# Local masks on VectorE, v's copies two half-steps later, and the third batch's scores in one group for each pair

## The chip, the core and the metric

The kernel runs on one core of a Trainium2 chip. The metric is the device time of one execution in microseconds, and the median over runs is what is compared. In this text PE is TensorE, DVE is VectorE, ACT is ScalarE, POOL is GpSimd and SP is SyncE, as the profile names them. One profiled execution supplies all times inside the kernel; they are counted from the start of its span.

## What is computed

Sparse attention over 8 batches of 8 heads (576 positions, head size 64) is followed by a two-layer block over the 4608 tokens. Heads 0 to 3 are local: a query sees its own key and the 31 before it. Heads 4 to 7 are strided: a query sees the earlier keys at its own position modulo 32.

```
scores = scale * q @ k.T                       # per batch and head
local   = (rel >= 0) & (rel < 32)              # heads 0..3, rel = query - key
strided = (rel >= 0) & (key % 32 == query % 32)  # heads 4..7
attn = softmax(where(mask, scores, -1e9));  x = attn @ v   -> (4608, 512)
h = x @ w_in                                   # 512 -> 2048
g = where(h > 0, h, exp(min(h, 0)) - 1)
out = g @ w_out                                # 2048 -> 512
```

## The kernel before, in words

**Two streams in one instruction order.** The two-layer block is done in 9 chunks of 512 tokens. Chunk `nb` has 16 steps `s`. A step multiplies 512 tokens by 128 columns of `w_in` (`moe_in`, four matmuls at L672), applies the activation (`moe_act`: the exponential on ACT at L698, then L705 and L707 on DVE), and does a quarter of one output block of `w_out` (`moe_out`, four matmuls at L721, mostly for the chunk before). The attention of batch `nb + 1` is laid between these pieces while chunk `nb` runs. Places between pieces are called gaps: gap `2s` is ahead of `moe_in` of step `s`, gap `2s + 1` is behind its `moe_act` and ahead of `moe_out`. The order on each engine is the order of emission, and an engine runs its instructions in that order.

**Opening and second batch.** The first batch is computed ahead of chunk 0 by a list, `OPENING`. The second batch (`b = 1`) lies in chunk 0 by the list `SECOND` of gap numbers and steps; `S0`, `S1` are its strided pairs of heads, `l0`, `l1` its local pairs. `t_q` and `t_k` are PE transposes with a copy out of PSUM, `s0`, `s1` the two halves of the scores, `a0`, `a1` the two halves of the product with v, `x` the transposition of the result into `xT`, and `halo` a copy inside v's local tile. `ON_VECTOR` names the copies that run on DVE; the others run on ACT.

**Later batches.** The third batch (`b = 2`, in chunk 1) follows `TIMES[2]`, whose pairs begin at gaps 4, 10, 15 and 21, strided pairs first. The offsets in the last tuple are for `t_q`, `t_k`, first scores, second scores, first product with v, second product, `x`, and `v_in`. `v_in` copies the strided v from `v_raw`, where a DMA has put it, to `v_str` in two parts on DVE (L439); only the first pair of a batch does it. For `b = 2` the transposes still run on PE; from `b = 3` they are DMA transposes.

**Scores and masks.** With `b < WHOLE`, `scores(u)` computes half of a pair's blocks into the two banks of `pair_a`, takes one exponential over them and, for `b = 2`, multiplies by the mask on DVE (`mask`, L556). With `b >= WHOLE`, `scores_all` computes all blocks of a pair at once, in `pair_a` and in two more banks of the ring; it takes one exponential (L488) and one mask product (L490) over `pair_a`, and `scores_rest` a gap later takes two short exponentials (L502) and one short mask product (L505) over the two other banks. For `b = FAR = 1` the mask is not a product: a matmul of the identity with `far_s` or `far_l` writes a large negative number to the masked places (L524), and the scores are added to it.

**Banks.** PSUM has 8 banks: the pair `pair_a`, two for `moe_in` (`half`), and four `single`. In chunk 1 three singles form the ring from which transposes, rest banks, products with v and `x` are taken in turn, and the fourth collects `moe_out`. `moe_in` of step `s + 2` needs the bank that L707 of step `s` has read.

**Loads.** q, k, v and the weights are loaded by DMAs that POOL issues. The order behind the opening is: the rest of `w_in`, four pieces of `w_out` (L790), then `load_batch(2)` (strided q, k, v at L192 and L196, then local q, k, v), then the memsets and `load_batch(3)`.

Of the kernel before, what the change touches and what calls it, by code (L numbers as in the profile page):

```python
# [11 lines left out]
BF16 = mybir.dt.bfloat16  # L12
I32 = mybir.dt.int32
ALU = mybir.AluOpType
# [10 lines left out]
LB = 96  # L25

L_RUN = 6
NEG = -1e30
# [5 lines left out]
TIMES = (  # L34
    None,
    None,
    ((4, 10, 15, 21), 0, (-3, -2, 0, 2, 4, 6, 9, 0)),
    ((2, 9, 15, 22), 0, (-2, -1, 0, 2, 3, 5, 8, 0)),
    ((2, 8, 15, 22), 0, PIECES),
)  # L40
# [3 lines left out]

SECOND = """
3 S0.t_k 5 S1.t_k 7 S0.s0 9 S0.s1 11 S1.s0 11 S0.a0 12 S0.a1 13 S1.s1 14 S1.a0 14 l0.t_q
16 S0.x 17 l0.t_k 17 S1.a1 19 l0.s0 19 l1.t_q 20 S1.x 20 S1.halo 21 l0.s1 21 l1.t_k 23 l1.s0
24 l0.a0 25 l0.a1 25 l1.s1 27 l1.a0 28 l0.x 28 l1.a1 31 l1.x
""".split()

# [4 lines left out]
s0.a0 l0.m1 l1.s0 s1.a1 s0.a1 s1.halo fill.1 l1.s1 l1.m0 l0.a0 fill.1 s1.x l1.m1 l0.a1 s0.x  # L55
fill.1 l1.a0 l1.a1 moe.2 l0.x moe.3 S0.t_q l1.x S1.t_q moe.0 moe.1
""".split()
ON_VECTOR = "s0.t_q s1.cast_q s1.t_k l0.t_q s0.v l1.x S1.t_q L1.t_k".split()


ON_SCALAR = (5, 7, 11, 15)
# [4 lines left out]
def kernel(  # L66
# [9 lines left out]
    nc = tc.nc  # L76
# [12 lines left out]
    consts = ctx.enter_context(tc.tile_pool(name="consts", bufs=1))  # L89
# [49 lines left out]
    identity = consts.tile([128, 128], BF16, tag="identity")  # L139
    mask_l = consts.tile([128, S], BF16, tag="mask_l")  # L140
    mask_w = consts.tile([128, 2 * 126 + 3 * 108], BF16, tag="mask_w")
    far_l = consts.tile([128, 3 * LB], BF16, tag="far_l")
    far_s = consts.tile([128, 126], BF16, tag="far_s")
    mask_s, mask_s3 = mask_w[:, 0:252], mask_w[:, 252:576]
    rden = consts.tile([128, B, 2, 2, 2, 6], F32, tag="rden")
# [25 lines left out]

    BY_DMA = 3

    WHOLE = 3

    FAR = 1
    RAW = 1
# [102 lines left out]
    for i in range(2):  # L280
# [19 lines left out]
                            op0=ALU.is_ge)  # L300
# [4 lines left out]
    for g in range(3):  # L305
# [8 lines left out]
                                   op0=ALU.is_le, op1=ALU.mult)  # L314
# [5 lines left out]

    nc.vector.tensor_scalar(far_s[0:126], mask_s[0:126, 0:126], scalar1=1.0,
                            scalar2=-NEG, op0=ALU.subtract, op1=ALU.mult)
    nc.vector.tensor_scalar(far_l, mask_l[:, 0:3 * LB], scalar1=1.0, scalar2=-NEG,
                            op0=ALU.subtract, op1=ALU.mult)

    load_strided(0, "k")
    load_local(0, "q")
# [26 lines left out]
    class Pair:  # L354
# [7 lines left out]
        def copy(self, step, late):  # L362

            if self.b < 2:
                name = self.name.upper() if self.b else self.name
                late = f"{name}.{step}" in ON_VECTOR
            return nc.vector.tensor_copy if late else nc.scalar.copy
# [139 lines left out]
        def scores(self, u):  # L507
            if self.b >= WHOLE:
                (self.scores_rest if u else self.scores_all)()
                return  # L510
            sc = rings["sc"].next()
            blocks = self.blocks(u)
            far = self.b == FAR
            if far:
                k, n = blocks[0][4:]
                g = len(blocks) // 2
                if self.strided:
                    t = far_s[0:k, 0:n].unsqueeze(1).to_broadcast([k, g, n])
                elif u == 0:
                    t = far_l  # L520
                else:
                    t = far_l[:, n:2 * n].unsqueeze(1).to_broadcast([k, g, n])
                for bank in range(2):
                    nc.tensor.matmul(sc[:, bank, 0:g * n], lhsT=identity[0:k, :],  # L524
                                     rhs=t, start=True, stop=False)
            for p, blk, bank, i, nk, nq in blocks:
                at, half = self.place(p, blk)
                d = slice(64 * half, 64 * half + 64)
                kind = "str" if self.strided else "loc"
                c = 0 if self.strided else LB * blk  # L530

                nc.tensor.matmul(sc[:, bank, i * nq:(i + 1) * nq],  # L532
                                 lhsT=kT[kind][self.b % 2][d, at, c:c + 128],
                                 rhs=qT[kind][self.b % 2][d, at, c:c + nq],
                                 start=not far,
                                 stop=not far or i == len(blocks) // 2 - 1)
            nk, nq = blocks[0][4:]
            w = len(blocks) // 2 * nq
            pr = (p_p if self.b else p_p0).tile([128, 1152 if self.b else 648], BF16, tag="pr", name="pr")
            halves = pr[0:nk, 0:2 * w].rearrange("k (a x) -> k a x", a=2)  # L540
            nc.scalar.activation(halves, sc[0:nk, :, 0:w], ACT.Exp, scale=scale)  # L541
            self.pr[u] = pr
            if self.b and not far:
                self.mask(u)
# [15 lines left out]
        def av(self, u):  # L560
# [8 lines left out]
            for p, blk, bank, i, _, _ in blocks:  # L569

                if self.b >= WHOLE:
                    pr, o, top = self.pr_all, self.probs[p, blk], 1152
# [70 lines left out]
    def attention(b, start, pitch, at):  # L643
# [6 lines left out]
        for i, pr in enumerate(pairs):  # L650
            for off, piece in ((at[0], pr.t_q), (at[1], pr.t_k),
                               (at[7], lambda pr=pr: pr.v_in(0)),
                               (at[7] + (b > 1), lambda pr=pr: pr.v_in(1)),
                               (at[2], lambda pr=pr: pr.scores(0)),
                               (at[3] if b < WHOLE else at[2] + (b < LATE),
                                lambda pr=pr: pr.scores(1)),
# [353 lines left out]
```

## Time and profile before

| What | Value |
|---|---|
| Median of 3 runs | 321.9 us (320.77, 321.9, 321.96) |
| Profiled execution, its own time | 322.11 us |
| Its span | 320.3 us |
| Granted PE clock | 0.997 |
| Busy: PE / DVE / ACT / POOL | 301.2 / 242.1 / 173.1 / 134.8 us |
| PE busy in 24.0 to 52.8 us | 26.70 of 28.80 us |
| PE busy in 52.8 to 88.0 us | 33.42 of 35.20 us |
| PE busy in 88.0 to 122.0 us | 33.78 of 34.00 us |

The profiled execution's own time is 1.8 us more than its span, which counts from the first to the last instruction. Chunk 0 of the two-layer block, with the second batch in its gaps, ends on PE at 52.84 us, where the first `moe_in` of chunk 1 starts; the third batch's attention lies in the gaps between there and 90.56 us, where chunk 2 starts. A duration in the tables of groups is the mean of one instruction. Matmuls follow one another faster than a single one lasts, so what a group of matmuls takes on PE is read from the start of its first to the start of what follows.

### The profile page before, as it was taken

How to read it: one execution, taken by the hardware profiler on the slowest of the kernel's cores; microseconds unless marked ns; L12 is line 12 of the kernel's file. 1: busy time of each engine (PE TensorE's matmuls, PEld its weight loads, DVE VectorE, ACT ScalarE, POOL GpSimd, SP SyncE). 2: the span in 40 equal slices, each digit the busy share in tenths (PEclk: the TensorE clock that was granted, in tenths of full speed). 3: DMA queues.
4: the chain of work that ended last, by engine and by line, in shares of the span. 5: the costliest groups of instructions: out<-in, count | busy, mean ns of one | idle time of the engine just before them, and what ended most of it. 6: DMA issues, size and time to landing. Idle time of an engine off the chain costs nothing.

```text
span 320.3 us, 6081 instructions
## 1 busy us (share of the span) xinstructions
PE 301.2 (94%) x2207; PEld 151.1 (47%) x2248; DVE 242.1 (76%) x542; ACT 173.1 (54%) x330; POOL 134.8 (42%) x213
## 2 busy tenths in 40 slices
PE   1899989899999999999999999999999999999994
PEld 0564545345444544444444544444445444444443
DVE  7787787487888988988798889887988666776610
ACT  3677876567455555456655655555565444434411
POOL 9666726959979658859733920000000000000000
PEclk9999999999999999999999999999999999999998
DMA  5999999999999999999997992571110000110012
GB/s 108 153 176 147 166 206 133 163 122 174 110 182 153 148 184 149 111 135 168 159 168 76 160 195 58 70 153 64 51 51 35 34 35 33 52 48 36 33 68 73
DMA packets 108971, 36.33 MB, mean 113 GB/s; under 512 B 87358, under 2 KB 104454, under 8 KB 108934
## 3 DMA queue, kind: packets, MB, share of 16 engines
q0 software_dynamic: 71632, 18.10, 63.7%
q1 hardware_dynamic: 37301, 17.77, 27.6%
q8 instruction: 19, 0.31, 0.4%
q14 instruction: 19, 0.15, 0.1%
HBM read 36.70 MB, written 9.44 MB: 144 GB/s over the span
## 4 chain that ended last, share of the span: by engine, by line
PE 78%; DMA 9%; DVE 6%; POOL 4%; issue 1%; ACT 1%; POOLq 0%; DVEq 0%; ACTq 0%
PE single L721 36%; PE half L672 25%; PE single L672 9%; DMA w_out_sb<-in_moe_w_out_dram 5%; PE single L577 3%; DMA k_loc<-in_k_dram 2%; PE pair_a L482 2%; DVE g_sb L707 2%; DMA v_raw<-in_v_dram 2%; DVE e_sb L705 1%; POOL k_str L192 1%; PE single L615 1%; PE single L400 1%; DVE x_l L588 1%; POOL w_out_sb L790 1%
## 5 line engine op out<-in xcount | busy, mean ns | idle before, releaser
L721 PE MATMUL single<-w_out_sb,g_sb 128*128 128x512 bf16 (+1 forms) x574 | 143.5, 373 | 1.1 <-issue 0.2
L672 PE MATMUL half<-xT,w_in_sb 128*128 128x512 bf16 x422 | 110.4, 379 | 1.9 <-DVE g_sb L707 1.1
L698 ACT ACTIVATE e_sb<-half 128x512 f32<-128x512 f32 x109 | 65.2, 599 | 73.5 <-PE half L672 70.4
L705 DVE TENSOR_SCALAR e_sb<-e_sb 128x512 bf16<-128x512 f32 x140 | 62.1, 444 | 35.5 <-ACT e_sb L698 34.8
L721 PEld LDWEIGHTS <-g_sb 128*128 128x128 bf16 x592 | 54.7, 98 | 56.2
L672 PEld LDWEIGHTS <-w_in_sb 128*128 128x128 bf16 x576 | 52.4, 98 | 57.5 <-issue 2.1
L707 DVE TENSOR_TENSOR g_sb<-e_sb,half 128x512 bf16<-128x512 bf16 x106 | 72.9, 688 | 3.7
L672 PE MATMUL single<-xT,w_in_sb 128*128 128x512 bf16 x133 | 35.8, 379 | 0.4
L698 ACT ACTIVATE e_sb<-single 128x512 f32<-128x512 f32 x35 | 21.1, 602 | 24.3 <-PE single L672 20.3
L726 ACT COPY o_sb<-single 128x512 f32<-128x512 f32 (+1 forms) x37 | 21.2, 574 | 17.3 <-PE single L721 16.9
L577 PEld LDWEIGHTS <-pr 128*128 128x128 bf16 (+3 forms) x352 | 20.7, 105 | 14.1 <-DVE pr L556 1.2
L488 ACT ACTIVATE pr<-pair_a 126x936 bf16<-126x936 f32 (+1 forms) x20 | 19.2, 962 | 11.9 <-PE single L482 11.9
L192 POOL DMA_DIRECT2D v_raw<-in_v_dram x32 | 20.0, 657 | 11.9 <-DVE v_str L439 11.7
L707 DVE TENSOR_TENSOR g_sb<-e_sb,single 128x512 bf16<-128x512 bf16 x34 | 23.4, 688 | 1.2
L192 POOL DMA_DIRECT2D k_str<-in_k_dram x32 | 19.6, 625 | 7.8 <-issue 3.1
L192 POOL DMA_DIRECT2D q_str<-in_q_dram x28 | 17.5, 643 | 5.5 <-DMA w_out_sb<-in_moe_w_out_dram 1.9
L588 DVE TENSOR_TENSOR x_l<-single,rden 96x384 bf16<-96x384 f32 x32 | 17.7, 553 | 1.1
L588 DVE TENSOR_TENSOR x_s<-single,rden 126x256 bf16<-126x256 f32 (+1 forms) x32 | 15.7, 491 | 1.1
L215 POOL DMA_DIRECT2D q_loc<-in_q_dram x20 | 15.7, 825 | 1.9 <-DMA k_str<-in_k_dram 1.9
L215 POOL DMA_DIRECT2D k_loc<-in_k_dram x20 | 15.3, 800 | 0.7 <-issue 0.4
L541 ACT ACTIVATE pr<-pair_a 128x576 bf16<-128x576 f32 (+2 forms) x20 | 13.0, 650 | 3.7 <-PE pair_a L532 3.5
L587 DVE RECIPROCAL rden<-single 96x6 f32<-96x6 f32 (+2 forms) x64 | 11.8, 185 | 2.4 <-PE single L577 1.9
(118 smaller groups left out, 254.9 us busy)
## 6 DMA issues: line engine op xcount, KB each, us to landing
out_dram<-o_sb SPq DMA_DIRECT2D x35, 256.0 KB, 2.6
v_loc<-in_v_dram POOLq DMA_DIRECT2D x8, 288.0 KB, 8.2
k_str<-in_k_dram POOLq DMA_DIRECT2D x32, 67.5 KB, 5.1
v_raw<-in_v_dram POOLq DMA_DIRECT2D x32, 67.5 KB, 5.0
w_in_sb<-in_moe_w_in_dram POOLq DMA_DIRECT2D x4, 512.0 KB, 8.0
w_out_sb<-in_moe_w_out_dram POOLq DMA_DIRECT2D x4, 512.0 KB, 12.5
q_str<-in_q_dram POOLq DMA_DIRECT2D x28, 67.5 KB, 6.9
q_loc<-in_q_dram POOLq DMA_DIRECT2D x20, 64.0 KB, 5.1
```

The costliest lines, as they stand in the source:

```text
L192: engine.dma_start(out=t[0:108, h].rearrange("p g d -> p (g d)"), in_=rows[h, :, 0:30, :].rearrange("t (r g) d -> t r (g d)", g=5))
L215: nc.gpsimd.dma_start(out=t[:, h // 2, 0:4, h % 2], in_=src[name][b, h, 0:512].rearrange("(i p) d -> p i d", p=128))
L488: nc.scalar.activation(both, sc[0:nk, :, 0:w], ACT.Exp, scale=scale)
L541: nc.scalar.activation(halves, sc[0:nk, :, 0:w], ACT.Exp, scale=scale)
L577: nc.tensor.matmul(to[:, 0:D] if apart else to, lhsT=pr[0:nk, o:o + m], rhs=vt[0:nk, 2 * self.hp + p, blk, :], start=True, stop=True)
L588: nc.vector.tensor_tensor(self.x[0:nq, b0:b0 + n].rearrange("q g p d -> q p g d"), av[0:nq, :, 0:n, 0:D], r.unsqueeze(3).to_broadcast([nq, ...
L672: nc.tensor.matmul(hps, lhsT=w_in_sb[:, c, m * 128:(m + 1) * 128], rhs=xT[:, c, nb * N_TILE:(nb + 1) * N_TILE], start=start, stop=stop)
L698: nc.scalar.activation(e_sb, hps, ACT.Exp)
L705: nc.vector.tensor_scalar(e1_sb, e_sb, scalar1=1.0, scalar2=1.0, op0=ALU.min, op1=ALU.subtract)
L707: nc.vector.tensor_tensor(g_of[nb][:, m, :], e1_sb, hps, op=ALU.max)
L721: nc.tensor.matmul(ops, lhsT=g_of[nb][:, m, kk * 128:(kk + 1) * 128], rhs=w_out_sb[:, m, cols], start=(m == 0), stop=(m == MC - 1))
L726: nc.scalar.copy(o_sb, ops)
```

## The change

Six things are different. `far_l` and the matmuls with it are gone, so that the second batch's local pairs get their mask by `mask` on DVE, as the third batch's do; its strided pairs keep `far_s`. `l1.t_k` of the second batch (`L1.t_k`) leaves `ON_VECTOR`, and its copy runs on ACT. `S1.x` and `S1.halo` move from gap 20 to gap 21. The third batch's `v_in` moves from offsets 0 and 1 to 2 and 3, which is from gaps 4 and 5 to gaps 6 and 7. `WHOLE` goes from 3 to 2, so that the third batch's scores go through `scores_all` and `scores_rest`. The tile `far_l` and the instruction that fills it are no longer there.

```
-    ((4, 10, 15, 21), 0, (-3, -2, 0, 2, 4, 6, 9, 0)),
+    ((4, 10, 15, 21), 0, (-3, -2, 0, 2, 4, 6, 9, 2)),
...
-16 S0.x 17 l0.t_k 17 S1.a1 19 l0.s0 19 l1.t_q 20 S1.x 20 S1.halo 21 l0.s1 21 l1.t_k 23 l1.s0
+16 S0.x 17 l0.t_k 17 S1.a1 19 l0.s0 19 l1.t_q 21 S1.x 21 S1.halo 21 l0.s1 21 l1.t_k 23 l1.s0
...
-ON_VECTOR = "s0.t_q s1.cast_q s1.t_k l0.t_q s0.v l1.x S1.t_q L1.t_k".split()
+ON_VECTOR = "s0.t_q s1.cast_q s1.t_k l0.t_q s0.v l1.x S1.t_q".split()
...
-    WHOLE = 3
+    WHOLE = 2
...
-    nc.vector.tensor_scalar(far_l, mask_l[:, 0:3 * LB], scalar1=1.0, scalar2=-NEG,
-                            op0=ALU.subtract, op1=ALU.mult)
...
-            far = self.b == FAR
+            far = self.b == FAR and self.strided
             if far:
                 k, n = blocks[0][4:]
                 g = len(blocks) // 2
-                if self.strided:
-                    t = far_s[0:k, 0:n].unsqueeze(1).to_broadcast([k, g, n])
-                elif u == 0:
-                    t = far_l
-                else:
-                    t = far_l[:, n:2 * n].unsqueeze(1).to_broadcast([k, g, n])
+                t = far_s[0:k, 0:n].unsqueeze(1).to_broadcast([k, g, n])
```

More of the change, by code (lines that the diff above doesn't have):

```diff
@@ L141 @@
     mask_w = consts.tile([128, 2 * 126 + 3 * 108], BF16, tag="mask_w")
-    far_l = consts.tile([128, 3 * LB], BF16, tag="far_l")
     far_s = consts.tile([128, 126], BF16, tag="far_s")
```

## The prediction

> **What bounds the kernel now.** I read the page's shares first, then the chain of work that ended last, in order of time, up to 66 us, then the timelines of PE and DVE over the same stretch, and last the groups of instructions by form. The shares of the chain:
>
> ```profile
> PE 78%; DMA 9%; DVE 6%; POOL 4%; issue 1%; ACT 1%; POOLq 0%; DVEq 0%; ACTq 0%
> ```
>
> Behind 64 us the chain is PE alone, matmul behind matmul. So a microsecond taken from PE there is a microsecond of the end, and one taken before is worth only what the last wait before 64 us lets through. That wait is in the chain (start, length, what):
>
> ```profile
> 36.49 15.22 DMA w_out_sb<-in_moe_w_out_dram
> ...
> 56.23 5.45 DMA v_raw<-in_v_dram
> ...
> 61.80 0.29 DVE v_str L439
> 62.09 0.33 DVE pr L556
> 62.42 0.35 DVE e_sb L705
> ...
> 62.79 0.70 DVE g_sb L707
> ...
> 63.53 0.38 PE half L672
> ```
>
> The third batch's v lands at 61.68 us, behind the weights, and its copy stands first on DVE, with a mask and an activation queued behind it. PE's and DVE's timelines show the same from both sides (the bracket is the idle time before):
>
> ```profile
> 55.23 0.43 PE L386 MATMUL single<-identity,k_str 126*128 126x126 bf16 x5 [0.23 <-DMA k_str<-in_k_dram]
> 62.48 0.33 PE L577 MATMUL single<-v_str,pr 126*128 126x65 bf16 x4 [0.67 <-DVE pr L556]
> 63.53 1.02 PE L672 MATMUL half<-xT,w_in_sb 128*128 128x512 bf16 x3 [0.46 <-DVE g_sb L707]
> 61.80 0.29 DVE L439 COPY v_str<-v_raw 126x512 bf16<-126x512 bf16 x1 [3.27 <-DMA v_raw<-in_v_dram]
> ```
>
> Two landings are thus dates that PE can't pass: 55.23 us for the key transposes, and v's. DVE sat idle for 3.27 us with work behind it. The prices come from the groups by form (busy, mean ns):
>
> ```profile
> L524 PE MATMUL pair_a<-far_l,identity 128*128 128x288 bf16 x8 | 1.6, 286 | 0.0
> L556 DVE TENSOR_TENSOR pr<-pr,mask_l 128x576 bf16<-128x576 bf16 x8 | 3.6, 450 | 0.0
> L403 DVE COPY kT_loc<-single 128x576 bf16<-128x576 bf16 x1 | 0.8, 751 | 0.0
> L488 ACT ACTIVATE pr<-pair_a 126x936 bf16<-126x936 f32 x10 | 9.5, 950 | 8.9 <-PE single L482 8.9
> L502 ACT ACTIVATE pr<-single 108x108 bf16<-108x108 f32 x20 | 4.0, 259 | 0.0
> L490 DVE TENSOR_TENSOR pr<-pr,mask_w 126x936 bf16<-126x936 bf16 x10 | 6.5, 646 | 5.1 <-ACT pr L488 5.1
> ```
>
> **The second batch, in chunk 0 (38 to 53 us).** PE loses four pairs of far_l matmuls. A pair holds PE for 0.34 us (39.29 to 39.63 us, and 41.85 to 42.19 us), so 1.36 us go, 0.34 of them ahead of a score matmul that waited 0.47 us for the key copy anyway. DVE gains four masks at 0.450, 1.80 us, and loses the key copy of 0.751: 1.05 us more. ACT gains that copy, 0.65 us at its own rate (L403 on ACT, 647 ns), ahead of the next exponential. I walked the three queues on from 38.4 us. PE first runs ahead by up to 1.1 us; then x of the first local pair waits for its normalisation, and the second half of the last pair's product with v waits for its mask at 48.85 us, where before it started at 48.83. The masks give back what the matmuls saved, and chunk 1 starts near 52.8 us, as before. The bounds are 51.5 us (all 1.36 kept) and 53.9 us (DVE's 1.05 all on PE). Either way little of it reaches the end: an early PE waits at 55.23 us for the keys, and a late one has 0.23 us there and some 0.65 us ahead of the product with v. I take 0, and a loss of 0.2 us at the late bound. S1.x at gap 21 takes away a 0.30 us wait for x_s (PE, 40.83 us), in the same cover. The filling of far_l (526 ns on DVE at 6.35 us) is hidden: PE's next steps there end on a landing of local keys at 13.86 us.
>
> **The first strided pair of the third batch (55 to 64 us).** From 55.23 us on I lay the new order out with the old durations. All scores at gap 4 take 0.36 us (the fourth batch's, 92.38 to 92.74 us) where two halves took 0.21 and 0.24. The exponential (0.95) and the mask (0.65) end at 59.4 us, the activation of step 2 at 60.5, the short mask at 60.8. DVE then stands before the copy of v from 60.8 to 61.8 us, with only step 3's activation behind it, whose exponential ends near 61. PE is at its first product with v at 61.5 us and waits for the copy alone: 61.80 + 0.29 + 0.06 gives 62.15 us instead of 62.48. The moe_in behind it needs the bank of step 2, which was free at 63.5 us and is now at 60.5, so the 0.46 us go too: 62.15 + 0.59 gives 62.74 us instead of 63.53. **Gain 0.79 us.** The second copy of v, at gap 7, stands behind step 3's activation and ends near 63.4 us; the second product with v comes at 64.4. The next product's normalisation follows it by 0.6 us.
>
> **The other three pairs (64 to 82 us).** Here PE is without waits, so its own time counts. Halves cost 0.45 (strided) or 0.46 us (local: 71.82 to 72.06 and 74.10 to 74.33), a group 0.36 (also local, 105.47 to 105.83): 0.1 each, 0.3 us. Ahead of a score group four large matmuls take 0.96 instead of 0.86 us (91.42 to 92.38 us against 93.61 to 94.47); the local pairs have one such place fewer each, 0.2 us. **Gain 0.5 us**, with bounds 0 and 0.75 (the last if the copies' slower products, 210 against 196 ns, go as well). ACT gets 0.95 + 2 times 0.26 where it had 0.59 and 0.71 us: 0.17 us a pair, beside idle time of over 1 us in six steps of that stage. DVE has the same elements in as many instructions.
>
> **Sum:** 322.11 - 0.79 - 0.5 = 320.8 us for the profiled execution, which stands 0.2 us above its median; for the median 321.9 - 1.3 = 320.6 us.
>
> **The rivals.** *The landings come earlier.* If PE's gain in chunk 0 holds and the landings aren't fixed dates, 1.36 + 0.30 us come on top: 319.0 us. For it: DMA share is 0.67 at 52 to 56 us, so the engines have room there. Against it: POOL is busy for 3.95 of those 4.00 us, and it issued k's remainder only when w_out had landed.
>
> *Nothing is gained, because v lands later.* The weights and loads ahead share the queues with outputs, and the profile can't say how fixed 61.68 us is. A microsecond later, plus a wait for a normalisation at gap 21, eats 1.3 us: 321.9 us. At gap 21 the first local pair's second product takes the bank of its first; before, that one was normalised at 79.22 us and PE came at 79.27.
>
> *VectorE locks GpSimd out.* Masks and copies on DVE would hold up POOL's writing of descriptors, so that v lands later by the four masks' 1.80 us: 322.11 + 1.80 - 1.29 = 322.6 us. Against it: in 37 to 52 us POOL waited for landings for some 10 us, which hides 1.8, and a mask beside busy POOL took 0.45 us (73.68 us) as one alone did. The Trainium skill (SBUF — State Buffer, "two separate sides") says that a DVE instruction in a two-port mode keeps GpSimd from writing DMA descriptors; copies in SBUF are of that kind, products of two tensors are not except against a GpSimd read. By that rule v's copies alone would matter, and they come when v's own issues are over.
>
> *Slower: two moe_in banks run short behind each group.* A long exponential and a long mask stand ahead of the activation that frees a bank. Behind the fourth batch's first group L707 ended at 95.73 us and its bank was needed at 96.33: 0.60 us to spare. In chunk 1, ACT has besides two copies out of PSUM for each pair (0.63 to 0.69 us) and the output copy (0.58 us), and the ring gives seven banks a pair instead of five. If both copies and an output copy fall between, 1.9 - 0.6 = 1.3 us are short, four times 5.2 us, or 2.6 us if at every second pair: 322.1 - 1.3 + 2.6 = 323.4, up to 326.0 us. It decides from L707 coming over 0.60 us later than there. Against it: the copies fall ahead of the pair's own group, a gap or more before.
>
> **How the numbers follow.** Measurements of this kernel tell about 0.5%, 1.6 us. The forecast (gain 0.5 to 2) gets 0.47, of which 0.15 lie beyond 1.6 us; earlier landings 0.20, nearly all of it beyond; nothing gained 0.12; the lock 0.05; slower by short banks 0.16, nearly all beyond 323.5 us. So faster 0.35, same 0.49, slower 0.16. The range, 319.0 to 323.4 us, leaves out the lower half of earlier landings and the upper half of short banks; the likeliest case alone has 319.9 to 321.4.
>
> **What would show it.** Right: no L524 with far_l; DVE's wait for v_raw falls from 3.27 to about 1 us and stands between the short mask and L439; PE's wait at the first product with v is for v_str, 0.3 to 0.7 us; the 0.46 us before moe_in is gone; PE waits about 0.2 us for k_str near 55.2 us. Wrong: chunk 1 starting after 53.7 us, v landing off 61.7 us by more than 0.5, or waits of moe_in for g_sb between 64 and 90 us.

## The result, and the profile after

The changed kernel's median is 319.67 us (22 runs, 318.57 to 322.71) against 321.41 us for the kernel before (22 runs, 319.99 to 322.54); the ratio is 0.9959 with a 95% interval of 0.994 to 0.9978. That is 1.3 us by the ratio and 1.7 us by the medians; forecast were 1.3 us and a ratio of 0.996. The profiled execution took 318.57 us, the fastest of its 22, where the one of before had taken 322.11 us, 0.7 us above its median. So the two profiles stand further apart (3.5 us) than the kernels do, and below every reading is made over several profiles.

The shares of the chain, from the page of the changed kernel:

```profile
PE 84%; DMA 6%; DVE 3%; POOL 2%; ACT 2%; issue 1%; POOLq 0%; ACTq 0%
```

PE has six points more, at the cost of DMA, DVE and POOL. PE's timeline has the same three places as before (start, length, work, and in brackets idle time ahead, of which there is none now):

```profile
54.01 0.44 PE L383 MATMUL single<-identity,k_str 126*128 126x126 bf16 x5
...
60.21 0.29 PE L569 MATMUL single<-v_str,pr 126*128 126x65 bf16 x4
60.34 0.43 PE L383 MATMUL single<-identity,k_str 126*128 126x126 bf16 x5
60.61 1.03 PE L664 MATMUL half<-xT,w_in_sb 128*128 128x512 bf16 x4
```

No 0.23 us for the keys, no 0.67 us at the product with v, no 0.46 us ahead of moe_in. DVE's timeline shows why:

```profile
57.51 0.65 DVE L487 TENSOR_TENSOR pr<-pr,mask_w 126x936 bf16<-126x936 bf16 x1 [0.38 <-ACT pr L485]
58.17 0.67 DVE L697 TENSOR_SCALAR e_sb<-e_sb 128x512 bf16<-128x512 f32 x1
58.87 0.69 DVE L699 TENSOR_TENSOR g_sb<-e_sb,half 128x512 bf16<-128x512 bf16 x1
59.48 0.26 DVE L502 TENSOR_TENSOR pr<-pr,mask_w 108x216 bf16<-108x216 bf16 x1
59.66 0.33 DVE L436 COPY v_str<-v_raw 126x512 bf16<-126x512 bf16 x1
```

Mask, activation and short mask now lie where DVE idled for 3.27 us, and the copy of v starts without a wait: v has landed by the time DVE comes to it. Chunk 0 has the local masks at the price that was taken from before, and the cost that the walk through the queues had found, x of the first local pair waiting for its normalisation (groups by form, and PE's timeline):

```profile
L548 DVE TENSOR_TENSOR pr<-pr,mask_l 128x576 bf16<-128x576 bf16 x8 | 3.6, 450 | 0.7 <-ACT pr L533 0.6
```

```profile
47.62 0.30 PE L620 MATMUL single<-identity,x_l 96*128 96x96 bf16 x3 [0.43 <-DVE x_l L580]
```

### The profile page after: what moved, and what is told of

Its sections match the earlier page's. It is cut to its first block, busy times and chain, and to the rows that moved or that the text cites. A ratio compares the mean times of both kernels' runs of the same rounds, so it can differ in the third digit from the quotient of the medians.

```text
span 316.8 us, 6114 instructions
## 1 busy us (share of the span) xinstructions
PE 299.8 (95%) x2240; PEld 149.1 (47%) x2240; DVE 242.6 (77%) x544; ACT 172.9 (55%) x335; POOL 137.5 (43%) x213
## 4 chain that ended last, share of the span: by engine, by line
PE 84%; DMA 6%; DVE 3%; POOL 2%; ACT 2%; issue 1%; POOLq 0%; ACTq 0%
PE single L713 39%; PE half L664 28%; PE single L664 9%; PE single L569 3%; DMA q_str<-in_q_dram 3%; PE pair_a L479 2%; DMA v_raw<-in_v_dram 2%; DMA k_str<-in_k_dram 2%; PE single L607 1%; ACT e_sb L690 1%; POOL k_str L191 1%; PE single L397 1%; DVE g_sb L699 1%; PE single L383 1%; DVE x_l L580 1%
## 5 line engine op out<-in xcount | busy, mean ns | idle before, releaser
L713 PE MATMUL single<-w_out_sb,g_sb 128*128 128x512 bf16 (+1 forms) x592 | 145.9, 373 | 0.0
L664 PE MATMUL half<-xT,w_in_sb 128*128 128x512 bf16 x436 | 112.6, 379 | 0.9 <-DVE g_sb L699 0.9
L697 DVE TENSOR_SCALAR e_sb<-e_sb 128x512 bf16<-128x512 f32 x140 | 62.5, 446 | 34.9 <-ACT e_sb L690 34.4
L699 DVE TENSOR_TENSOR g_sb<-e_sb,half 128x512 bf16<-128x512 bf16 x106 | 72.9, 688 | 3.7
L664 PE MATMUL single<-xT,w_in_sb 128*128 128x512 bf16 x140 | 36.5, 379 | 0.0
L485 ACT ACTIVATE pr<-pair_a 126x936 bf16<-126x936 f32 (+1 forms) x24 | 23.1, 961 | 12.4 <-PE single L479 11.9
L569 PEld LDWEIGHTS <-pr 128*128 128x128 bf16 (+3 forms) x352 | 20.0, 101 | 13.7 <-issue 1.3
L699 DVE TENSOR_TENSOR g_sb<-e_sb,single 128x512 bf16<-128x512 bf16 x34 | 23.4, 688 | 1.2
L191 POOL DMA_DIRECT2D k_str<-in_k_dram x32 | 21.1, 698 | 6.8 <-issue 2.6
L191 POOL DMA_DIRECT2D v_raw<-in_v_dram x32 | 20.7, 683 | 5.0 <-DVE v_str L436 3.7
L569 PE MATMUL single<-v_loc,pr 128*128 128x65 bf16 x192 | 11.6, 195 | 0.8 <-ACT v_loc L444 0.3
```

The source lines that it names most:

```text
L191: engine.dma_start(out=t[0:108, h].rearrange("p g d -> p (g d)"), in_=rows[h, :, 0:30, :].rearrange("t (r g) d -> t r (g d)", g=5))
L485: nc.scalar.activation(both, sc[0:nk, :, 0:w], ACT.Exp, scale=scale)
L569: nc.tensor.matmul(to[:, 0:D] if apart else to, lhsT=pr[0:nk, o:o + m], rhs=vt[0:nk, 2 * self.hp + p, blk, :], start=True, stop=True)
L664: nc.tensor.matmul(hps, lhsT=w_in_sb[:, c, m * 128:(m + 1) * 128], rhs=xT[:, c, nb * N_TILE:(nb + 1) * N_TILE], start=start, stop=stop)
L697: nc.vector.tensor_scalar(e1_sb, e_sb, scalar1=1.0, scalar2=1.0, op0=ALU.min, op1=ALU.subtract)
L699: nc.vector.tensor_tensor(g_of[nb][:, m, :], e1_sb, hps, op=ALU.max)
```

## The experiments

Theory D is the prediction's: v's landing holds up DVE, and the change gains by taking DVE's other work out from behind it, with 0.5 us of PE time beside. Rivals came up on the way: that only PE's own time counts (P), that grouping is the whole gain (G), that tile addresses set the landings (A).

Medians of these kernels scatter. The kernel before, run as one of the experiments, gave a ratio to itself of 0.9977 (0.9948 to 1.0005); its median of 12 was 320.58 us against 321.0 us. Differences of parts, 0.1 to 0.4%, can't be told by medians of 12. So the stretches of each profile are read as well, from one profile for each kernel:

- **chunk 0**: from the first far_s matmul of the second batch to the first moe_in of chunk 1
- **first pair**: from the third batch's first key transposes to the fifth moe_in of chunk 1
- **other pairs**: from there to the fourth batch's first scores
- **v behind keys**: from the third batch's first key transposes to the landing of the last of the five loads of v

| Kernel | masks on DVE | v moved | grouped | chunk 0 | first pair | v behind keys | DVE's wait for v | other pairs | ratio to before |
|---|---|---|---|---|---|---|---|---|---|
| before | no | no | no | 23.98 | 8.30 | 6.4 | 3.27 | 28.85 | |
| b0_before_again | no | no | no | 24.23 | 8.29 | 6.4 | 3.31 | 28.85 | 0.9977 (0.9948 to 1.0005) |
| x2_far_l_last | no | no | no | 24.49 | 8.06 | 6.0 | 2.96 | 28.85 | 1.0033 (1.0004 to 1.0063) |
| e5_before_v_early | no | no | no | 23.57 | 6.84 | not read | 0 | 28.97 | 0.998 (0.9958 to 1.0003) |
| e3_masks_only | yes | no | no | 23.04 | 7.83 | 5.8 | 2.60 | 28.85 | 0.9992 (0.997 to 1.0014) |
| e2_v_moved_only | no | yes | no | 24.23 | 7.06 | 5.7 | 0.29 | 28.64 | 0.9991 (0.9968 to 1.0014) |
| e8_no_grouping | yes | yes | no | 23.42 | 7.06 | 5.7 | 0.11 | 28.77 | 0.9992 (0.9964 to 1.0021) |
| e1_whole_only | no | no | yes | 24.62 | 8.11 | 6.0 | 3.04 | 28.60 | 0.996 (0.994 to 0.9979) |
| e1b_whole_again | no | no | yes | 23.58 | 6.60 | 3.2 | 0 | 28.29 | 0.9994 (0.9966 to 1.0022) |
| after | yes | yes | yes | 23.35 | 6.60 | 5.1 | 0 | 28.54 | 0.9959 (0.994 to 0.9978) |
| e4_after_again | yes | yes | yes | 23.04 | 6.82 | 5.0 | 0 | 28.07 | 0.9981 (0.996 to 1.0003) |
| x1_hole | yes | yes | yes | 24.78 | 7.18 | 5.7 | 0 | 28.25 | 0.9965 (0.994 to 0.9991) |
| e6_after_v_early | yes | yes | yes | 23.44 | 7.14 | not read | 0 | 28.06 | 0.997 (0.9942 to 0.9998) |
| b1_v_at_7_8 | yes | later | yes | 23.25 | 8.32 | 7.2 | 0 | 28.06 | 0.9985 (0.9953 to 1.0016) |

### The three parts alone, and the whole again

**Grouping only:**

```
-    WHOLE = 3
+    WHOLE = 2
```

> The kernel before, with only the third batch's scores in one group for each pair. Theory D (v's landing is a date near 61.7 us, and before it time saved on PE is lost): DVE's mask over the whole group stands behind the waiting copy of v, so the first product with v starts about 0.3 us later than before (62.8 instead of 62.5), and the other three pairs bring 0.5 us: 0.2 to 0.3 us faster than before. Theory P (what counts is PE's own time wherever it lies): four pairs at about 0.19 us, 0.75 us faster.

**The copies of v only:**

```
-    ((4, 10, 15, 21), 0, (-3, -2, 0, 2, 4, 6, 9, 0)),
+    ((4, 10, 15, 21), 0, (-3, -2, 0, 2, 4, 6, 9, 2)),
```

> The kernel before, with only the third batch's copies of v at gaps 6 and 7. Theory D: the mask and the activation no longer stand behind the copy; the first product with v waits for the copy alone, and the wait for a moe_in bank is gone: 0.8 us faster than before. Theory P: no instruction of PE is saved, a wait only changes its name: 0, or at most the 0.3 us at the first product.

**The second batch's part only** (the whole change, with these two lines as before):

```
-    WHOLE = 2
+    WHOLE = 3
-    ((4, 10, 15, 21), 0, (-3, -2, 0, 2, 4, 6, 9, 2)),
+    ((4, 10, 15, 21), 0, (-3, -2, 0, 2, 4, 6, 9, 0)),
```

> The kernel before, with only the second batch's part: local masks on DVE, its last key copy on ACT, S1.x and S1.halo one gap later, far_l gone. Theory D: chunk 1 starts between 0 and 1 us earlier, and the wait for v at the first product takes it back: 0 (from -0.2 to +0.2 us). Theory P: up to 1.0 us faster, as much as chunk 1 starts earlier.

**The changed kernel again**, no edit:

> The changed kernel once more, beside its parts on one chip. Theory D: 1.3 us faster than before, more than the sum of what masks and grouping bring alone, since the two need the copy of v out of the way. Theory P: the sum of the three parts. Both: DVE's wait for v is under 1 us; where v lands early it is 0, and the time is then nearer to 319 us.

By medians the surprise was grouping alone: 319.76 us against 321.18, 1.4 us, where D had expected 0.2 to 0.3 and P 0.75; its interval (0.7 to 1.9 us) leaves out D's figure. v moved alone and masks alone read 0.3 us by their ratios, with intervals too wide to tell D from P. The whole read 0.6 us, below P's sum of the three (1.8 us) and with D's 1.3 us at the edge of its interval. The stretches speak for D: grouping takes the other pairs from 28.85 to 28.60 us and leaves the first at 8.11 us. Moving v takes the first pair from 8.30 to 7.06 us, but v also landed 0.7 us sooner behind the keys there. The time of e1's own profile, 322.47 us, was its slowest, so its median wasn't explained by it; hence the repeat below.

### Grouping taken away, and a second time alone

```
-    WHOLE = 2
+    WHOLE = 3
```

> The changed kernel with the third batch's scores in halves again (masks on DVE and copies of v moved stay). Theory D: the stretch from the fifth moe_in of chunk 1 to the fourth batch's first scores is 28.85 us (in five profiles with halves 28.6 to 29.0, in five with groups 28.1 to 28.6), and the time is about 0.5 us above the changed kernel's. Theory G (grouping is the whole gain, as its median alone, 1.4 us below, suggests): the time of the kernel before.

> The kernel before with only the grouping, a second time. Theory D: 0.25 to 0.75 us faster than before; its first median, 1.4 us, was luck with landings. Theory G: 1.3 us faster again.

The second run of grouping alone gave 0.9994 (0.9966 to 1.0022): 0.2 us, so the first 1.4 us was at least in part luck, and G's 1.3 us lies outside the second interval (up to 1.1 us). The mean of the two ratios, 0.9977, is still 0.7 us: by medians alone grouping could be half of the gain or more, and what limits it is the stretches. Without grouping the other pairs take 28.77 us, as D says, and the ratio to before is 0.9992, nearer to G's "time of the kernel before" than to D's 0.5 us above the changed kernel; its interval, 0.6%, holds both. Over all profiles the other pairs take 28.64 to 28.97 us in halves (seven, mean 28.83) and 28.06 to 28.60 us in groups (seven, mean 28.27): grouping is worth 0.56 us there on average, whatever else is changed.

### The kernel before as its own control

No edit.

> The kernel before itself, as a null run beside the others. All theories: 0. If its median differs from the other runs of the same kernel by 0.2% or more, differences of that size between kernels here are scatter of the loads' landings and not an effect; the kernel with far_l placed last, which differs in no instruction, read 0.33% slower.

0.23% off itself: that is the scatter. It bears on the next experiment too, whose 0.33% "slower" is no more than this and a little.

### Do tile addresses set the landings?

In the first six profiles one load told the kernels with far_l from those without. POOL issues the third part of w_in near 24 us, and stands before v_loc until it is there: in all fourteen profiles it starts v_loc 0.55 to 0.56 us after that landing. From the rows of DMA issues between 23.3 and 25.9 us (size, us from issue to landing), kernel before:

```profile
w_in_sb<-in_moe_w_in_dram POOLq DMA_DIRECT2D x1, 512.0 KB, 7.7
```

and the changed kernel:

```profile
w_in_sb<-in_moe_w_in_dram POOLq DMA_DIRECT2D x1, 512.0 KB, 5.4
```

Without far_l every later tile moves down by its 576 bytes a partition. One edit of the changed kernel puts the gap back, one edit of the kernel before takes it out of the constants:

```
+    hole = consts.tile([128, 3 * LB], BF16, tag="hole")
+    nc.vector.memset(hole[0:1, 0:2], 0.0)
     far_s = consts.tile([128, 126], BF16, tag="far_s")
```

> The changed kernel with far_l's 576 bytes a partition kept as an unused tile in its old place (one tiny memset on it), so that every tile has the address that it had before. In the three profiles with the local masks on DVE the w_in load that POOL issues near 24 us lands 5.4 to 5.7 us later, in the three others 7.6 to 7.7 us. Theory A (the tiles' addresses set how fast the loads land): it lands after 7.6 us again, POOL's wait before v_loc near 30 us is 2 to 3 us again, v lands near 61.7 us, and the time is 1 us or so above the changed kernel's. Theory F (far_l's fill on DVE, or the work on DVE, sets it): it stays at 5.5 us and the time is the changed kernel's.

```
-    far_l = consts.tile([128, 3 * LB], BF16, tag="far_l")
...
+    far_l = consts.tile([128, 3 * LB], BF16, tag="far_l")
     stage = {n: p_g.tile([128, 4, 5, D], F32, tag="g_sb", name=f"{n}_stage")
```

> The kernel before with the far_l tile placed behind the other constant tiles: v_loc, v_str and the q and k tiles have the changed kernel's addresses, v_raw, pr and g_sb those of before; no instruction differs. Theory A: the w_in load near 24 us lands after 5.5 us, v lands 1 to 2 us earlier, and the time falls by 0 to 1 us; if v_raw's address is what matters, no change. Theory F: 7.6 us as before, the same time as before.

With the hole the load took 8.1 us, as A had it, but the time stayed with the changed kernel's (0.9965). With far_l last it took 7.8 us; A was left only with v_raw's address. Then the changed addresses gave 7.8 us in e6 and 7.3 in e8, and the old ones 6.2 us in e5 and in e1b. The same layouts give both: in fourteen profiles it lands after 5.4 to 6.5 us in six and 7.3 to 8.1 us in eight, and neither the addresses nor far_l's fill sets which. Theory A falls. What sets it stays open; six profiles that sorted perfectly were chance.

### The landing taken away

The third batch's copies read v of the batch before, which landed near 33 us; the third batch's strided part has the wrong v.

```
-                i = rows_of(raw[self.b], slice(0, 4))[part]
+                i = rows_of(raw[1 if self.b == 2 else self.b], slice(0, 4))[part]
```

> The kernel before, but the third batch's v copies read the second batch's v_raw, which landed near 33 us, so that the third batch's strided part uses the wrong v and no copy waits for a landing. Theory D (v's landing is what chunk 1 waits for): DVE's 3.3 us of idle time goes, PE's 0.67 and 0.46 us go: 1.1 us faster than before, perhaps a little more where v lands late. Theory P: at most 0.3 us faster.

> The changed kernel with the same edit (the third batch's copies read the second batch's v_raw). Theory D: what is left of the wait for v in the changed kernel goes, 0 to 0.5 us against the changed kernel, so it is 0.3 to 0.8 us ahead of the kernel before with the same edit: what masks and grouping bring without v's date. Theory P: the same distance from that kernel as between the changed kernel and the one before, 1.3 us.

The first pair falls from 8.30 to 6.84 us in the kernel before: 1.46 us, more than D's 1.1. In the changed kernel it stays at 7.14 us, within the 6.60 to 7.18 us of that kernel with its own v. So in these profiles, where v landed up to 5.7 us behind the keys, the landing costs it nothing any more. In ratios the two are 0.998 and 0.997, 0.3 us apart, the low end of D's 0.3 to 0.8 and below P's 1.3; the intervals overlap so far that they don't rule P out. e1b agrees without an edit: there v was in time at gap 4 (copy at 59.67 us, no wait), and the first pair took 6.60 us with the copy in its old place.

### The copies another gap later

```
-    ((4, 10, 15, 21), 0, (-3, -2, 0, 2, 4, 6, 9, 2)),
+    ((4, 10, 15, 21), 0, (-3, -2, 0, 2, 4, 6, 9, 3)),
```

> The changed kernel with the third batch's copies of v another gap later, at gaps 7 and 8, right ahead of the products that read them. Theory D: where v lands after 60 us, step 3's activation no longer stands behind the copy, but the first product waits for the same landing: 0 to 0.2 us faster than the changed kernel, with 0 the likelier. Theory G: 0. If the copy now comes behind step 3's activation on DVE, the first product starts up to 1 us later when v has landed early: then slower by that.

The first pair is back at 8.32 us, as if the expectation's last sentence had come true. PE's and DVE's timelines of this kernel:

```profile
61.85 0.30 PE L569 MATMUL single<-v_str,pr 126*128 126x65 bf16 x4 [1.33 <-DVE v_str L436]
```

```profile
58.32 1.19 DVE L697 TENSOR_SCALAR e_sb<-e_sb 128x512 bf16<-128x512 f32 x1
59.54 0.69 DVE L699 TENSOR_TENSOR g_sb<-e_sb,half 128x512 bf16<-128x512 bf16 x1
60.15 0.26 DVE L502 TENSOR_TENSOR pr<-pr,mask_w 108x216 bf16<-108x216 bf16 x1
60.33 0.47 DVE L697 TENSOR_SCALAR e_sb<-e_sb 128x512 bf16<-128x512 f32 x1
60.83 0.69 DVE L699 TENSOR_TENSOR g_sb<-e_sb,half 128x512 bf16<-128x512 bf16 x1
61.50 0.59 DVE L436 COPY v_str<-v_raw 126x512 bf16<-126x512 bf16 x2
```

The copies stand behind step 3's activation, and PE waits 1.33 us for them. But the chain that ended last does not run through the activation:

```profile
55.81 5.57 DMA v_raw<-in_v_dram
...
61.50 0.31 DVE v_str L436
61.85 0.30 PE single L569 x4
```

v landed at 61.38 us in this run, and the copy starts 0.12 us later, as it does in the seven profiles of the table where DVE waited for v. The activation ended at 61.52 us, just when the copy could start anyway. So the wait is v's, which landed later behind the keys than in any other profile, and not the placement's. An estimate says the same: by the prediction's layout (copy 0.12 us behind the landing, 0.29 and 0.06 us to the product, 0.59 us to moe_in) a copy at gap 6 would have given 7.2 + 1.1 = 8.3 us. The median, 320.92 us (0.9985), lies between the two kernels. What a gap later costs where v lands early is not shown; gap 4 is shown to be too early. No tried version has a lower ratio than the changed kernel.

## Why the prediction was right, and where it was off

**The size and the sign** came out as forecast: ratio 0.996 predicted, 0.9959 measured. So close a hit is in part luck: the same kernel again gave 0.9981 (0.996 to 1.0003), the forecast median, 320.6 us, is 0.9 us above the measured one, and the terms behind it came out less evenly.

**The first strided pair, 0.79 us.** The mechanism held: DVE's idle time before the copy (2.6 to 3.3 us in the five profiles with v at gap 4 and late) is 0 to 0.29 us in the six with v at gap 6, and the 0.46 us for a moe_in bank are gone. On average the first pair takes 8.12 us in those five and 6.98 in those six, 1.14 us less. Not all of that is the change's: v also landed sooner behind the keys, 5.0 to 5.7 us where the five have 5.8 to 6.4 (the sixth, e6, doesn't read it). Where v landed alike, 5.7 to 5.8 us behind the keys, the first pair takes 7.83 us with gap 4 (e3) and 7.06 to 7.18 us with gap 6 (e2, e8, x1). That is 0.65 to 0.77 us, near the forecast, and e3 and e8 differ in nothing but v's copies. The second wait of 1 us that the prediction left DVE at gap 6 came to 0.29 us at most. DVE reached the copy 5.4 to 6.2 us behind the keys, where 5.6 were laid out, but v was there by then, and not 6.4 us behind them.

**Two fixed dates** is the step that failed. The keys were used at 54.01 us without a wait, and v landed at 59.06 us; in the kernel before run again, v landed at 62.47 us. The landings move by up to 3.5 us from run to run. Of the prediction's signs, v's landing off 61.7 us by more than 0.5 was one of being wrong, and it came; of those of being right, the waits of PE for the keys and for v_str and the 1 us of DVE did not come. The forecast's other case, "the landings come earlier", is nearer to the profiled run of the changed kernel (318.57 us) in time, though not in its term, since chunk 0 gave 0.4 to 0.6 of its 1.36 us. Its 319.0 us is the forecast median less 1.66 us; counted from the profiled 320.8 us it is 319.1. Over all runs the median lies between the two cases.

**The second batch, 0.** The walk found the right waits (0.43 us for the normalisation), but gave back too much: chunk 0 takes 23.04 to 24.78 us with masks on DVE (seven profiles, mean 23.47) and 23.57 to 24.62 us without (seven, mean 24.10). Chunk 0 is also shorter where the third part of w_in lands sooner, and of the eight slower loads (7.3 to 8.1 us) five fall to the kernels with far_l. Beside slower loads alone the means are 23.88 and 24.31 us, beside faster ones 23.17 and 23.58: about 0.4 us were saved, within the stated bounds.

**The other pairs, 0.5 us:** 0.56 us by the stretches, the best-sized term.

**The terms don't add up to the whole.** As averages 0.6, 1.14 and 0.56 us make 2.3 us, where the ratio gives 1.3. At like landings 0.4, 0.7 and 0.56 us make 1.7 us, an estimate, and 1.7 us is also what the medians give. The profiled runs of the kernel before, 322.11 and 322.79 us, are above that kernel's median, those of the changed one (318.57, 319.67 and, with the hole, 320.67 us) around its own. When v lands in time, as in e1b, the first pair's part isn't there to be gained. What lies outside the stretches scatters as well: the start up to the first far_s matmul takes 27.9 to 30.2 us, and the part from the fourth batch's first scores to the end 227.4 to 228.8 us. What each term brings to the median is thus argued from the profiles, not measured run by run.

**The rivals.** Short moe_in banks: PE's waits of the changed kernel between 36 and 92 us are these two, and neither is for g_sb:

```profile
PE pair_a L524 <- ACT kT_loc L400: 0.5, 1, 0.5
PE single L620 <- DVE x_l L580: 0.4, 1, 0.4
```

The reuse of a ring bank at gap 21 cost nothing either. *Nothing gained because v lands later* did not happen in the changed kernel's profiles, but b1's late v shows what it would cost: a first pair of 8.32 us, as before the change. VectorE locking GpSimd out so that v lands late: v landed no later in the changed kernel, but a lock showed up the other way round (below), and on an activation, where the prediction had counted v's copies alone.

## What to carry to other kernels

In an in-order queue, an instruction that waits for a DMA should stand behind the work that doesn't need the data, as far as what needs it allows: two half-steps too early cost 0.65 to 0.77 us here where the data landed equally late. Before a wait is put down to the placement, look when the data landed: in the version with the copies a gap later the order looked guilty, and the landing was. A landing in one profile is a sample and not a date: run the unchanged kernel as a control, and when medians scatter by 0.2%, read the same stretch in several profiles. A saving on an engine with a wait behind it is worth only what that wait lets through in the run at hand.

## What the runs showed of the hardware

**An activation on DVE that starts well inside a long DMA issue on POOL waits for its end; one that starts right behind the issue's start doesn't.** L697 (L705 before) takes 0.44 to 0.45 us on average. In the changed kernel with the hole, where it is L699, it took 1.18 us; DVE's and POOL's timelines:

```profile
59.46 1.18 DVE L699 TENSOR_SCALAR e_sb<-e_sb 128x512 bf16<-128x512 f32 x1
```

```profile
59.20 1.18 POOL L204 DMA_DIRECT2D v_loc<-in_v_dram  x1
```

POOL's issue of v_loc ends at 60.38 us, DVE's instruction at 60.64, 0.26 us later. The same pair ends 0.25 us apart in after, e6, b1 and e1b, with DVE starting 0.4 to 1.1 us before POOL's end and taking 0.67, 1.14, 1.19 and 1.30 us. In the kernel before DVE idled in front of v's copy then, so the change moved an activation under this issue.

An earlier pair of the changed kernel shows the other case, with DVE starting 0.21 us behind POOL:

```profile
29.93 0.42 DVE L697 TENSOR_SCALAR e_sb<-e_sb 128x512 bf16<-128x512 f32 x1
```

```profile
29.72 1.44 POOL L202 DMA_DIRECT2D v_loc<-in_v_dram  x1 [0.68 <-DVE e_sb L697]
```

Here DVE is not held, and POOL's issue, 1.2 us elsewhere, ends 0.81 us behind it. Over the v_loc issues of all fourteen profiles, the seven activations that started in the first 0.23 us of an issue took 0.42 to 0.43 us, and the issue ended 0.81 us behind each of them. The 36 that started 0.25 us or more into it, and more than 0.21 us ahead of its end, ended 0.22 to 0.26 us behind the issue and took up to 1.30 us.

The masks, products of two tensors, kept their 0.450 us. The Trainium skill (SBUF — State Buffer, "two separate sides") says that the port pair which VectorE and GpSimd share is an exclusive lock held for a whole instruction, and that whoever starts first blocks the other; this trace agrees, with GpSimd as the one that came first in the long activations.

**Loads issued in the same order land up to 2.7 us apart in different runs** (5.4 to 8.1 us for one 512 KB load), and the kernel before against itself reads 0.9977.
